# Seven matrix products that nobody reads, ahead of the first keys

## The chip, the cores and the metric

The kernel runs on one core of one Trainium2 chip. The metric is device time in microseconds (us). A profile of one execution goes with the times. TensorE (PE, with its weight loads as PEld), VectorE (DVE), ScalarE (ACT) and GpSimd (POOL) each have their own queue of instructions; SyncE (SP) mostly issues loads and stores.

## What is computed

The reference runs a decaying linear attention and then an FNet block, all in float32. Sizes are B = 4 batches, H = 8 heads, S = 768 positions, D = 64, so the model width is 512, and the MLP width is 2048.

```python
for b in range(nb):                       # blocks along the sequence
    intra = einsum('bhic,bhjc->bhij', qb, kb) * Dmask
    intra = einsum('bhij,bhjd->bhid', intra, vb)
    inter = einsum('bhid,bhde->bhie', qb * lam_pow, kv_state)
    out[:, :, sl] = intra + inter
    kv_state = lam_block * kv_state + einsum('bhsd,bhse->bhde', kb_dec, vb)
# x = out as (B, S, H*D)
mixed = real(fft(fft(x, axis=1), axis=2))
u = x + mixed
un = (u - mean) / sqrt(var + 1e-6)
y = u + maximum(un @ w_ch1, 0) @ w_ch2
```

`w_ch1` and `w_ch2` arrive as float64 and are turned into float32 on the chip.

## The kernel before

The work is written as Python generators that yield now and then; `weave` and `beside` run several of them side by side, so that the instructions of the attention, of the Fourier mixing, of the weight conversion and of the MLP are mixed in the program. A scheduler then orders the instructions of each engine by its own estimate of when things are ready. An instruction wrapped in `tc.keep_in_program_order` keeps its place. On each engine the instructions run in the order that results.

**Front.** The decay factor `lam` is loaded, an identity `ident` is built by GpSimd, and VectorE makes two tables out of them with scans: `decay` (L160, one scan for each of eight heads) and `qpow` (L167, four scans). Every score product is multiplied by `decay`.

**Attention.** A batch goes through six chunks of 128 positions. For each chunk `attn_in` (L259) loads k, q and v in pieces of 64 floats for one head and position, transposes k (L274) and q (L279) on TensorE against `ident`, and ScalarE copies the results out of PSUM as kT (L276) and qT (L281). GpSimd multiplies k by the decay (`kd`, L270); VectorE makes `qs` (L285). `attn_out` (L289) then multiplies kT and qT to scores (L298), VectorE applies the decay (`sc`, L302), the state gets kd times v (L315, and L317 or L320), and the output is summed from qs times the old state (L328) and sc times v (L332). ScalarE copies it out as `oT` (L335), TensorE turns it back (L348), and ScalarE writes x (L352, L353). The buffers of k, q and v are double, so a load waits until the chunk two before is used up. All the loads go through the sync queue, in order.

**Weights.** `load_weights` (L200) loads a piece of 512 columns of float64 as pairs of 32-bit words (`raw`, L209) and makes floats of it in seven instructions: two on ScalarE (L216, L218) and five on VectorE (L217, L220, L222, L224, L225). The two engines hand the piece to each other: L217 (VectorE), then L218 (ScalarE), then L220 (VectorE), and L216 (ScalarE) before L220. The pieces are woven between the chunks of batch 0 and the stages after it.

```python
pin(nc.scalar.activation(sg, top.bitcast(I16), AF.Sign))                      # L216
pin(nc.vector.tensor_scalar(pw, top, 0x7FF0, None, op0=ALU.bitwise_and))      # L217
nc.scalar.activation(pw, pw, AF.Relu, bias=cvt[:, 0:1], scale=8.0)            # L218
nc.vector.tensor_tensor(p, p, sg, op=ALU.mult)                                # L220
pin(nc.vector.tensor_scalar(d, hi, 0x000FFFFF, 0x00100000, ...))              # L222
nc.vector.scalar_tensor_tensor(dst, lo, 2.0 ** -32, d, ...)                   # L224
nc.vector.scalar_tensor_tensor(dst, dst, 2.0 ** -20, p, ...)                  # L225
```

**Mixing and MLP.** VectorE folds the rows (L426 to L484), TensorE does the two transforms (L516, then L529 to L534), VectorE adds the result to x (L596 to L600), takes mean and variance (L546, L547), GpSimd the power (L550, L551), and VectorE writes the normalised rows `un` (L564). TensorE transposes them (L569) and ScalarE copies them to `ut` (L570), the input of the MLP, whose first product is L633 and whose second is L647. The PSUM pool `pa` (five banks) serves the attention and the mixing; the pool `pm` (three banks), from which `psum_m` takes its tiles, serves the MLP alone. The later part of the MLP is computed with fewer products in a second phase (L720, L767).

The order of the main stages around the change is written in the last lines:

```python
run(part(att0, 2.7))
run(beside(att0, NC * t_chunk - 2.7, w, 0.25 * NW))
run(beside(part(mix, T_FOLD), T_FOLD, att1, 3.25 * t_chunk))
```

Of the kernel before, what the change touches and what calls it, by code (L numbers as in the profile page):

```python
# [76 lines left out]
def kernel(  # L77
# [10 lines left out]
    nc = tc.nc  # L88
# [50 lines left out]
    def new(pool, shape, tag, **kw):  # L139
        cnt[0] += 1  # L140
        return pool.tile(shape, F32, tag=tag, name=f"{tag}{cnt[0]}", **kw)
# [4 lines left out]
    def psum_m(shape):  # L146
        return new(pm, shape, "pm")
# [6 lines left out]
    ident = const.tile([128, 128], F32, name="ident")  # L154
# [17 lines left out]
    nc.gpsimd.memset(cvt, -896.0 * 16 * 8)  # L172
    mhalf = const.tile([128, G], F32, name="mhalf")
    nc.gpsimd.memset(mhalf, -0.5)

    st = [const.tile([128, HP, D], F32, name=f"st{i}") for i in range(2)]

# [725 lines left out]
```

## Time and profile before

| | |
|---|---|
| time, median of 3 | 826.14 us (825.62 to 828.82) |
| span of the profiled execution | 824.8 us |
| TensorE busy | 798.2 us |
| VectorE busy | 437.8 us |
| ScalarE busy | 186.5 us |
| first TensorE instruction | 4.68 us |
| first `oT` copy | 13.97 us |
| first normalised rows (`un`) | 91.99 us |

The first rows say how full each engine is over the whole run. A busy share of the whole run is a mean over stages that differ, so the stages are looked at one by one: the first 100 us hold attention, mixing and weight conversion, where several engines take part; after that TensorE has the MLP. The last three rows are marks in time by which two profiles can be compared.

### The profile page before, as it was taken

To read this page: it belongs to the slowest core of one execution; us is meant where nothing else is said; L and a number is where in the kernel's file an instruction comes from. 1 tells how busy PE (TensorE), PEld (TensorE's weight loads), DVE (VectorE), ACT (ScalarE), POOL (GpSimd) and SP (SyncE) were. 2 spreads that over 40 slices of the span, in tenths; PEclk is the share of its full clock that TensorE was granted. 3 is DMA by queue.
4 is the path that set the end of the run, shared out by engine and by line. 5 is a ranking of instruction groups with operands and counts; after the bars stand their busy time and mean duration, and the time that the engine had idled before them with its cause. 6 is when DMAs were issued, how large, how long until landed. Compare 5 with 4: busy or idle time off the path is not lost.

```text
span 824.8 us, 11701 instructions
## 1 busy us (share of the span) xinstructions
PE 798.2 (97%) x4608; PEld 637.5 (77%) x4608; DVE 437.8 (53%) x1018; ACT 186.5 (23%) x448; POOL 78.4 (10%) x102
## 2 busy tenths in 40 slices
PE   7989799999999999999999999999999999999998
PEld 5767675758575857768748888888888888888886
DVE  6899779685745571345895541155313561146311
ACT  3755243324521211212102210022001220012100
POOL 3123310011110110220100000000000000000000
PEclk9999899999999999999999999999999999999999
DMA  9969343238842137530442011100111001110010
GB/s 240 259 132 280 98 152 99 83 75 202 212 116 68 55 74 141 128 120 2 115 115 89 1 52 51 52 1 0 54 50 52 0 1 39 33 33 0 1 39 25
DMA packets 126684, 68.88 MB, mean 84 GB/s; under 512 B 111150, under 2 KB 112174, under 8 KB 126630
## 3 DMA queue, kind: packets, MB, share of 16 engines
q1 hardware_dynamic: 121488, 55.67, 26.6%
q0 software_dynamic: 2112, 6.69, 2.5%
q10 hardware_dynamic: 3030, 5.78, 2.0%
q8 instruction: 36, 0.59, 0.3%
q14 instruction: 18, 0.15, 0.1%
HBM read 48.72 MB, written 19.40 MB: 83 GB/s over the span
## 4 chain that ended last, share of the span: by engine, by line
PE 81%; DVE 9%; issue 4%; DMA 3%; ACT 2%; POOL 1%; POOLq 0%; ACTq 0%; DVEq 0%; SPq 0%
PE p L767 23%; PE p L720 23%; PE pm L647 10%; PE pm L633 8%; PE pa L332 3%; PE pa L298 3%; PE pa L516 3%; PE pa L328 2%; DMA raw<-in_moe_w_ch_dram 2%; PE pa L274 1%; PE pa L315 1%; PE pa L348 1%; PE pa L279 1%; DMA x<-xb,ix 1%; DVE sc L302 1%
## 5 line engine op out<-in xcount | busy, mean ns | idle before, releaser
L633 PE MATMUL pm<-ut,w 128*128 128x256 f32 x512 | 119.9, 383 | 0.0
L647 PE MATMUL pm<-w,hr 128*128 128x512 f32 x256 | 115.8, 597 | 0.6 <-DVE w L225 0.6
L633 PEld LDWEIGHTS pm<-ut,w 128*128 128x128 f32 x512 | 94.2, 190 | 15.8 <-issue 4.1
L720 PE MATMUL p<-ur,w 128*128 128x256 f32 x384 | 93.8, 379 | 0.0
L647 PEld LDWEIGHTS pm<-w,hr 128*128 128x128 f32 x256 | 46.7, 190 | 50.0 <-issue 47.8
L720 PEld LDWEIGHTS p<-ur,w 128*128 128x128 f32 x384 | 73.0, 190 | 10.3 <-issue 0.5
L720 PE MATMUL p<-us,w1s 128*128 128x256 f32 x256 | 65.7, 379 | 0.0
L767 PE MATMUL p<-w,hs 128*128 128x256 f32 x256 | 58.0, 379 | 0.5 <-DVE y L788 0.5
L767 PE MATMUL p<-w2s,hs 128*128 128x256 f32 x256 | 57.9, 379 | 0.0
L767 PE MATMUL p<-w,ha 128*128 128x256 f32 x256 | 57.9, 379 | 0.0
L767 PEld LDWEIGHTS p<-w,hs 128*128 128x128 f32 x256 | 48.5, 190 | 7.5 <-DVE y L788 0.9
L767 PEld LDWEIGHTS p<-w2s,hs 128*128 128x128 f32 x256 | 48.6, 190 | 6.6
L767 PEld LDWEIGHTS p<-w,ha 128*128 128x128 f32 x256 | 48.6, 190 | 6.6
L720 PEld LDWEIGHTS p<-us,w1s 128*128 128x128 f32 x256 | 48.6, 190 | 6.6
L747 ACT COPY ha<-p 128x256 f32<-128x256 f32 x32 | 11.9, 372 | 169.1 <-PE p L720 139.4
L622 POOL DMA_INDIRECT out_dram<-y,ix x12 | 11.8, 988 | 402.4 <-DVE y L793 341.6
L758 DVE TENSOR_TENSOR ha<-p,ha 128x256 f32<-128x256 f32 x32 | 13.6, 425 | 45.2 <-ACT ha L757 45.2
L298 PEld LDWEIGHTS pa<-qT,kT 64*128 64x128 f32 x384 | 26.8, 198 | 12.8 <-ACT qT L281 6.7
L302 DVE TENSOR_TENSOR sc<-pa,decay 128x512 f32<-128x512 f32 x48 | 31.5, 683 | 8.2 <-PE pa L298 8.2
L332 PE MATMUL pa<-sc,v 128*64 128x128 f32 x384 | 32.3, 286 | 3.1 <-DVE sc L302 3.0
L298 PE MATMUL pa<-qT,kT 64*128 64x128 f32 x384 | 31.5, 297 | 2.9 <-ACT qT L281 2.6
L720 PE MATMUL p<-us,w 128*128 128x256 f32 x128 | 32.9, 379 | 0.0
(144 smaller groups left out, 1122.1 us busy)
## 6 DMA issues: line engine op xcount, KB each, us to landing
raw<-in_moe_w_ch_dram SPq DMA_DIRECT2D x32, 512.0 KB, 4.6
k<-in_k_dram SPq DMA_DIRECT2D x24, 256.0 KB, 5.0
q<-in_q_dram SPq DMA_DIRECT2D x24, 256.0 KB, 5.9
v<-in_v_dram SPq DMA_DIRECT2D x24, 256.0 KB, 4.9
ud<-x SPq DMA_DIRECT2D x16, 256.0 KB, 2.3
utd<-e SPq DMA_DIRECT2D x64, 64.0 KB, 2.2
u<-ud SPq DMA_DIRECT2D x16, 256.0 KB, 2.7
ur<-utd SPq DMA_DIRECT2D x6, 512.0 KB, 4.4
```

The lines of the kernel that those rows point to most:

```text
L298: mm(pss[hi][:, hp, :], lhsT=kT[HD[hi], hp, :], rhs=qT[HD[hi], hp, :], start=True, stop=True)
L302: nc.vector.tensor_tensor(t, pss[hi], decay[:, hi::2, :], op=ALU.mult)
L328: mm(po[HD[hi], hp, :], lhsT=s_old[HD[hi], hp, :], rhs=qs[HD[hi], hp, :], start=(hp == 0), stop=False, skip_group_check=True)
L332: mm(po[HD[hi], hp, :], lhsT=vt[:, 2 * hp + hi, :], rhs=sc[hi][:, hp, :], start=(c == 0 and hp == 0), stop=(hp == HP - 1), skip_group_chec ...
L516: mm = nc.tensor.matmul(ps[0:m, n, :], lhsT=piece(a, i, n), rhs=cs[0:rows, a, i in (2, 3), n, :], start=(a == 0), stop=(a == 1))
L622: nc.gpsimd.indirect_dma_start(out=out.rearrange("b s d -> (b s) d"), out_offset=row_of(2 + HC * (b + 1) + T - HC), in_=y[:, :], in_offset ...
L633: nc.tensor.matmul(ps, lhsT=w1[:, c, 128 * fc:128 * fc + 128], rhs=ut[:, c, :], start=(c == 0), stop=(c == KO - 1))
L647: nc.tensor.matmul(ps, lhsT=hr[(fc - f0) // 4][:, fc % 4, 128 * i:128 * i + 128], rhs=w2[:, fc, :], start=(fc == f0), stop=(fc == f1 - 1))
L720: nc.tensor.matmul(ps, lhsT=s2.A[a][:, kt, 128 * i:128 * i + 128], rhs=U[b][:, kt, :], start=(first and kt == 0), stop=(kt == 1), skip_gro ...
L747: nc.scalar.copy(a11, two(X))
L758: V.tensor_tensor(a22, two(Z), a22, op=ADD)
L767: nc.tensor.matmul(ps, lhsT=h[a][:, s, i, :], rhs=s2.B[b][:, i, :], start=(first and i == 0), stop=(i == HF - 1), skip_group_check=True)
```

## The change

Ahead of the attention, TensorE is given seven products of the identity with itself. Their result goes to a PSUM tile of the MLP's pool and is read by nothing. The products keep their place in the program, ahead of the first transposes of the keys. They are meant for the time in which the first keys are still on their way and TensorE has nothing to do: the array is to be at its full clock when the keys come.

```diff
     mhalf = const.tile([128, G], F32, name="mhalf")
     nc.gpsimd.memset(mhalf, -0.5)
+
+
+    idle = psum_m([128, 128])
+    for _ in range(7):
+        tc.keep_in_program_order(nc.tensor.matmul(idle, lhsT=ident, rhs=ident, start=True, stop=True))
 
     st = [const.tile([128, HP, D], F32, name=f"st{i}") for i in range(2)]
```

The diff shows all that was written. The scheduler decides the rest: with the seven products in the program it also places many other instructions of the first 117 us elsewhere, on all engines. After L174 the line numbers of the changed kernel are higher by five.

## The prediction

> **What bounds the kernel now.** I read the engine totals first, then the windows by stage, then the chain of waits and the timelines of the front. On the page:
>
> ```profile
> PE 798.2 (97%) x4608; PEld 637.5 (77%) x4608; DVE 437.8 (53%) x1018; ACT 186.5 (23%) x448; POOL 78.4 (10%) x102
> ```
>
> TensorE is busy for 798.2 of 824.8 us, so at most 26.6 us of idle time, plus slow matmuls, can be gained at all. The windows by stage say where:
>
> ```profile
> 20.00:40.00 20.00, 18.26 (x228) 15.17 (x227) 17.25 (x33) 14.24 (x33) 4.64 (x5) 1.00 1.02 258
> 40.00:60.00 20.00, 17.50 (x213) 13.79 (x214) 19.65 (x40) 11.92 (x30) 4.20 (x4) 1.00 0.72 152
> 80.00:120.00 40.00, 34.77 (x258) 28.14 (x257) 29.74 (x70) 16.87 (x40) 10.06 (x12) 0.91 0.45 132
> ```
>
> The columns are span, length, busy time of PE, PEld, DVE, ACT, POOL, then clock, DMA share, GB/s. Between 20 and 60 us VectorE is as full as TensorE (17.25 and 19.65 of 20 us), so a faster TensorE alone gives little there. From about 94 us, when the MLP has its first input, TensorE nearly always has work. A front that ends earlier pays only by what it moves the first normalised rows, at 91.99 us. The chain of waits in the front:
>
> ```profile
> 0.73 3.82 DMA k<-in_k_dram
> 4.55 0.14 issue
> 4.68 1.08 PE pa L274 x4
> 5.80 1.13 PE pa L279 x4
> 6.95 0.59 ACT qT L281
> 7.59 2.08 PE pa L298 x16
> 9.67 1.05 PE pa L315 x16
> 10.72 0.42 PE pa L332 x2
> 11.14 1.05 PE pa L274 x4
> 12.19 1.76 PE pa L332 x14
> 13.97 0.58 ACT oT L335
> ```
>
> It is TensorE nearly alone, and slow: L298 takes 2.08 us here and 1.16 at 15.71 us, L332 x14 1.76 against 1.10 at 19.16. Single L332 records shrink from 421 to 273 ns near 13.5 us. The page prints clock 1.00 in this stretch, so the durations, not that column, show that the array starts slow.
>
> **What the Trainium skill says.** "TensorE: Matmul & The Clock Gate", section "Part 1: The HAM clock gate", says that the array starts at half clock, that a busy window of about 3413 ns releases it, and that the windows run free of the kernel's start. This trace agrees: clock 0.50 from 92.14 to 98.97 us (6.83 us, two such windows), and counting windows of 3.413 us back from 98.97 gives 13.63, 10.22, 6.81 and 3.39 us, where 13.63 fits the shrinking records. The window 6.81 to 10.22 was some 80% busy (gap 6.91 to 7.59) and released nothing; 10.22 to 13.63 was full and did. The same page, under "Architectural detail", has ScalarE and VectorE as strict FIFO, which every step below uses; ScalarE standing 4.20 us at a weight word (shown below) agrees. "DMA: Bandwidth & Descriptors", section "Specifications", asks 512 B or more for line rate; 111150 of the 126684 packets here are under that, so the loads of the front are slow to land.
>
> **The change, part by part.** Line numbers are those of before.
>
> Added: seven f32 products of 128x128. A plain f32 product is two records (L529: two per call), 0.43 us at the low clock (L529 x2 at 95 us), so 7 x 0.43 = 3.0 us. They wait only for the identity (GpSimd, done at 1.67 us) and so run from about 1.7 to 4.75 us, beside the k load that ends at 4.55. The k transposes start perhaps 0.07 us later; that is hidden, since the q transposes wait for their own load until 5.79. Their PSUM buffer is first wanted at 100 us: nothing.
>
> Gained at the front: TensorE is now busy from 1.7 to 6.9 us, so the full window 3.39 to 6.81 releases the clock 6.8 us earlier. Then qT is copied at about 6.5, L298 runs 7.1 to 8.3. VectorE is busy with the scans until 6.99+2.16 = 9.15 us, so the first score product moves only from 9.70 to 9.15. The second ends at 10.45, k transposes fit before it, and L332 x14 ends at 11.7 instead of 13.95. ScalarE then has to fit L218 before oT, so VectorE's L220 comes at 13.5 instead of 15.22: 1.7 us gained. Bounds: 1.1 (release late) to 2.2 (TensorE's own gain).
>
> Moved: the scheduler orders much of the first 117 us anew; after that the built orders agree but for few places. Three moves matter.
>
> (1) VectorE's L217 on the third weight word goes ahead of L224 and qs of the third chunk. That word lands late:
>
> ```profile
> 21.19 0.69 DVE L224 SCALAR_TENSOR_TENSOR w<-raw,w 128x512 f32<-128x512 uint32 x1
> 21.98 0.69 DVE L285 TENSOR_TENSOR qs<-pa,qpow 128x512 f32<-128x512 f32 x1
> 22.80 0.67 ACT L216 ACTIVATE e<-raw 128x512 bf16<-128x512 int16 x1 [0.31 <-DMA raw<-in_moe_w_ch_dram]
> ```
>
> It lands at 22.74 us. Its issue, in the sync queue behind a v load, can move up by at most 1.1 us (that load waits from 12.83 to 13.96 for TensorE), with the DMA share near 1 all the while. So it lands at 21.6 to 22.7, VectorE stands there for 2 us or more, and behind it queue L224, qs, L225, L220, L222, sc, L224: with the step from the landing some 4.0 us to the second sc, at 25.7 to 26.7 us against 25.39. The gain of 1.7 us is spent, and 0.3 to 1.3 us more. TensorE's L328 and L332 wait for that.
>
> (2) Later in batch 0 other words are converted earlier, and k transposes and kT go ahead of oT. By the last chunk VectorE has 4.67-2.56 = 2.1 us less left between second sc and qs, so the lag is made up: about level, give or take 0.6 us, at 52 us.
>
> (3) The weight load that stands at 61.18 us is put ahead of the v load that held it in the queue:
>
> ```profile
> 60.70 0.37 SPq L263 DMA_DIRECT2D v<-in_v_dram  x1
> 61.18 0.52 SPq L209 DMA_DIRECT2D raw<-in_moe_w_ch_dram  x1
> 67.12 0.66 ACT L216 ACTIVATE e<-raw 128x512 bf16<-128x512 int16 x1 [4.20 <-DMA raw<-in_moe_w_ch_dram]
> 67.69 0.57 ACT L335 COPY oT<-pa 128x512 f32<-128x512 f32 x1
> 68.31 0.66 PE L348 MATMUL pa<-ident,oT 128*128 128x128 f32 x4 [1.04 <-ACT oT L335]
> ```
>
> It can now issue at 57.5 and land at 57.5+5.9 = 63.4. ScalarE no longer holds oT from 66.25 to 67.69: 1.4 us. VectorE's L217 for it now stands before the scores and may wait some 0.3 us, and VectorE's folds then bind, with 2.6 us of work from L470 to the next scores. I credit 0.8 us.
>
> Sum at the first normalised rows: level after (2), less 0.8, and 0.3 for small idle times of VectorE that close (0.46 at 20.2, 0.75 at 79.5 us): 1.1 us earlier. 826.14 - 1.1 = 825.0 us.
>
> **The rivals.**
>
> A, the front gain is spent and the rest is small: 825.0 (824 to 826.5). For it: VectorE full from 20 to 60 us. Against: that same VectorE idles 3.01 us before 15.22, which the change does attack.
>
> B, faster by over 0.5%. The weight word lands as early as VectorE wants it, so the 1.7 us last, and 0.8 comes at 68. Besides, TensorE now idles from 88.25 to 92.55 us, one whole window (88.73 to 92.14) lies in it, and the clock falls:
>
> ```profile
> 88.25:92.50 4.25, 0.01 (x1) 0.00 (x0) 3.32 (x9) 0.80 (x3) 1.29 (x2) 0.96 1.12 272
> 92.50:99.00 6.50, 5.94 (x34) 5.35 (x34) 2.56 (x7) 1.67 (x5) 3.14 (x3) 0.50 0.35 95
> ```
>
> From 94.15 to 98.97 the chain is TensorE, 4.8 us at half clock. If the moved idle no longer covers a window, half of that goes: 2.4 us. 826.1 - 1.7 - 0.8 - 2.4 = 821.2. Against: three things must go well.
>
> C, the words land late at further places where L217 now stands earlier (fourth and fifth chunk): 0.5 us at each of three, so about 827.6.
>
> D, slower by over 0.5%: the 1.3 us of step (1) stays, and stalls open one more idle window of 3.41 us in which nothing comes to TensorE: 826.1 + 1.3 + 3.4 = 830.8. Against: 18.26 of 20 us are busy from 20 to 40 us.
>
> **How the numbers follow.** A 0.55, C 0.12, B 0.22, D 0.11. A is the likeliest: 825.0. Same is A and C, 0.67; faster 0.22; slower 0.11. The range 821.0 to 829.5 cuts about half of B and most of D, which is the 2 in 10.
>
> **What would show it.** In the changed profile 14 identity records from 1.7 to 4.8 us; L298 of the first chunk near 1.2 us long; oT of the first chunk about 1 us earlier or more; ScalarE's L216 or VectorE's L217 waiting for a weight word near 21 to 23 us; ScalarE's wait of 4.20 us before 67 us gone or short; the first un within 2 us of 91.99. I am wrong if L298 stays at 2 us (no release), if VectorE does not stand near 22 us (B), or if the half-clock stretch at 92 us is gone.

## The result, and the profile after

The changed kernel takes 830.78 us (median of 6; 829.41 to 835.1) against 825.81 us for the kernel before beside it: ratio 1.0063, 95% interval 1.0036 to 1.0091. It is slower by about 5 us, where 1 us faster was forecast. Of all executions below one, of e1 at 1378.73 us with a mean clock of 0.56, was in a slow state and is left out of its ratio. Line numbers of the changed kernel are higher by five, so L303 below is L298 of before, L307 is L302 (`sc`), L222 is L217.

The engine totals of the changed kernel, and its windows by stage (span, length, busy time of PE, PEld, DVE, ACT, POOL, clock, DMA share, GB/s):

```profile
PE 803.4 (97%) x4622; PEld 641.8 (77%) x4622; DVE 439.7 (53%) x1018; ACT 186.8 (23%) x448; POOL 78.7 (9%) x102
```

```profile
20.00:40.00 20.00, 17.08 (x212) 13.84 (x212) 16.98 (x34) 14.19 (x33) 4.59 (x4) 1.00 0.98 251
40.00:60.00 20.00, 17.93 (x208) 14.06 (x206) 19.03 (x38) 11.55 (x29) 3.35 (x4) 1.00 0.63 138
80.00:120.00 40.00, 34.56 (x263) 28.66 (x262) 28.56 (x66) 18.14 (x44) 8.54 (x11) 0.91 0.45 125
```

From 20 to 40 us TensorE does 16 matmuls fewer than in the kernel before and is busy 1.2 us less. The chain of waits in the front of the changed kernel:

```profile
1.22 4.93 DMA q<-in_q_dram
6.15 0.04 issue
6.19 1.13 PE pa L284 x4
7.32 0.02 issue
7.34 0.59 ACT qT L286
7.94 0.04 issue
7.98 2.13 PE pa L303 x16
```

The 14 identity records run from 1.73 us and delay nothing: the chain goes past them, to the load of q. But L303 takes as long as L298 did, 2.1 us, so the array is still slow at 10 us. Further on, VectorE from 20 us (start, duration, engine, line, operation, and the wait before it), and last the second `sc` of this chunk in the kernel before:

```profile
20.07 0.41 DVE L227 TENSOR_SCALAR w<-raw 128x512 uint32<-128x512 uint32 x1
22.36 0.43 DVE L222 TENSOR_SCALAR e<-raw 128x512 uint16<-128x512 uint16 x1 [1.87 <-DMA raw<-in_moe_w_ch_dram]
22.70 0.68 DVE L229 SCALAR_TENSOR_TENSOR w<-raw,w 128x512 f32<-128x512 uint32 x1
23.30 0.68 DVE L290 TENSOR_TENSOR qs<-pa,qpow 128x512 f32<-128x512 f32 x1
...
26.64 0.68 DVE L307 TENSOR_TENSOR sc<-pa,decay 128x512 f32<-128x512 f32 x1
```

```profile
25.39 0.68 DVE L302 TENSOR_TENSOR sc<-pa,decay 128x512 f32<-128x512 f32 x1
```

That is the forecast wait, and the second `sc` at 26.64 us, in the foreseen 25.7 to 26.7. The weight load that stood at 61.18 us, and ScalarE behind it, also went nearly as foreseen: ScalarE's wait of 4.20 us is 0.43 (lines of the timeline, sync queue and ScalarE).

```profile
58.66 0.81 SPq L214 DMA_DIRECT2D raw<-in_moe_w_ch_dram  x1
...
64.87 0.67 ACT L221 ACTIVATE e<-raw 128x512 bf16<-128x512 int16 x1 [0.43 <-ACT x L358]
```

What was not foreseen comes after. These are windows of the changed kernel, cut at the clock's own borders (its records have the clock released at 11.00 us, and half from 75.86 to 79.27 us and from 96.34 to 103.16 us):

```profile
4.18:7.59 3.41, 3.03 (x13) 2.04 (x11) 3.41 (x10) 0.83 (x2) 0.72 (x1) 1.00 1.18 266
7.59:11.00 3.41, 3.02 (x33) 2.79 (x34) 2.18 (x5) 0.34 (x1) 0.36 (x1) 1.00 1.34 251
72.44:75.86 3.42, 1.73 (x18) 1.32 (x19) 3.42 (x9) 0.83 (x2) 0.47 (x2) 1.00 1.06 304
75.86:79.27 3.41, 3.41 (x14) 3.31 (x14) 2.80 (x6) 1.69 (x4) 3.28 (x1) 0.50 0.82 173
```

A window in which TensorE was busy for 1.73 of 3.41 us, VectorE for all of it, was followed by one at half clock. TensorE stood there for VectorE (timeline of the changed kernel, and last the same `sc` in the kernel before):

```profile
71.70 1.27 DVE L484 TENSOR_TENSOR fo<-fo 65x255 f32<-65x255 f32 x1
72.90 0.41 DVE L485 TENSOR_TENSOR fo<-fo 65x255 f32<-65x255 f32 x1
73.23 1.28 DVE L307 TENSOR_TENSOR sc<-pa,decay 128x512 f32<-128x512 f32 x2
...
73.97 0.43 PE L337 MATMUL pa<-sc,v 128*64 128x128 f32 x2 [1.57 <-DVE sc L307]
```

```profile
71.14 1.28 DVE L302 TENSOR_TENSOR sc<-pa,decay 128x512 f32<-128x512 f32 x2
```

The lag, mark by mark, with four of the experiments below (each column is one profiled execution; us against the profile of before):

| mark (time before) | change | e7, change again | e2 | e3 | e12 |
|---|---|---|---|---|---|
| scores of the second chunk (15.71) | -0.66 | -1.93 | -0.42 | -1.89 | -1.76 |
| first `sc` of batch 1 (52.56) | +1.19 | +2.21 | +2.00 | +0.45 | -0.27 |
| `sc` of its fourth chunk (71.14) | +2.09 | +3.12 | +2.92 | +1.36 | +0.31 |
| first `un` (91.99) | +3.97 | +3.32 | +3.12 | +1.57 | +0.51 |

So the front is early at 16 us, as foreseen but by less in this profile, late at 52 us, where level was foreseen, and later still at 72 and 92 us.

### The profile page after: what moved, and what is told of

Read it like the earlier page. It is cut to its first block, busy times and chain, and to the rows that moved or that the text cites. A ratio compares the mean times of both kernels' runs of the same rounds, so it can differ in the third digit from the quotient of the medians.

```text
span 829.6 us, 11732 instructions
## 1 busy us (share of the span) xinstructions
PE 803.4 (97%) x4622; PEld 641.8 (77%) x4622; DVE 439.7 (53%) x1018; ACT 186.8 (23%) x448; POOL 78.7 (9%) x102
## 4 chain that ended last, share of the span: by engine, by line
PE 78%; DVE 10%; DMA 4%; issue 4%; ACT 2%; POOL 1%; SPq 0%; POOLq 0%; ACTq 0%; DVEq 0%
PE p L772 23%; PE p L725 23%; PE pm L652 9%; PE pm L638 8%; PE pa L521 3%; PE pa L337 3%; PE pa L303 2%; DMA raw<-in_moe_w_ch_dram 2%; PE pa L333 1%; PE pa L353 1%; PE pa L279 1%; DVE sc L307 1%; DMA x<-xb,ix 1%; DVE w L229 1%; PE pa L320 1%
## 5 line engine op out<-in xcount | busy, mean ns | idle before, releaser
L303 PEld LDWEIGHTS pa<-qT,kT 64*128 64x128 f32 x384 | 27.3, 198 | 12.0 <-ACT qT L286 6.2
L307 DVE TENSOR_TENSOR sc<-pa,decay 128x512 f32<-128x512 f32 x48 | 31.4, 683 | 7.5 <-PE pa L303 7.4
L303 PE MATMUL pa<-qT,kT 64*128 64x128 f32 x384 | 32.0, 298 | 2.1 <-ACT qT L286 2.1
L337 PEld LDWEIGHTS pa<-sc,v 128*64 128x64 f32 x384 | 23.1, 136 | 13.4 <-DVE sc L307 7.5
```

The source lines that it names most:

```text
L303: mm(pss[hi][:, hp, :], lhsT=kT[HD[hi], hp, :], rhs=qT[HD[hi], hp, :], start=True, stop=True)
L307: nc.vector.tensor_tensor(t, pss[hi], decay[:, hi::2, :], op=ALU.mult)
L337: mm(po[HD[hi], hp, :], lhsT=vt[:, 2 * hp + hi, :], rhs=sc[hi][:, hp, :], start=(c == 0 and hp == 0), stop=(hp == HP - 1), skip_group_chec ...
```

## The experiments

**Theory.** The products cost nothing by themselves; the new order costs, where conversion work and its waits stand ahead of the decay products `sc`. **Rival 1**: work of TensorE ahead of the keys costs by itself, through the clock. **Rival 2**: the half-clock window at 76 us is all of it. Times are medians; each kernel was measured beside the kernel before on the same chip, and the ratio is to that. The kernel before had 825.81 (change), 826.50 (e1 to e4), 826.21 (e5 to e7), 826.39 (e8 to e11) and 826.64 us (e12 to e14), so times from different groups can differ by 0.8 us for the chip alone.

| run | us | ratio (95% interval) |
|---|---|---|
| e1 work, old order | 829.29 | 1.0037 (1.0024 to 1.0050) |
| e2 one product | 829.79 | 1.0045 (1.0032 to 1.0058) |
| e3 third piece pinned | 828.51 | 1.0030 (1.0016 to 1.0044) |
| e4 narrow products | 826.18 | 0.9996 (0.9986 to 1.0007) |
| e5 tile alone | 826.30 | 1.0009 (0.9997 to 1.0021) |
| e6 float32 products, old order | 826.84 | 1.0009 (0.9997 to 1.0022) |
| e7 change again | 832.56 | 1.0075 (1.0048 to 1.0101) |
| e8 18 products, old order | 827.92 | 1.0023 (1.0012 to 1.0033) |
| e9 e8 and third piece pinned | 827.47 | 1.0016 (1.0004 to 1.0028) |
| e10 third piece pinned alone | 825.97 | 0.9996 (0.9985 to 1.0006) |
| e11 e1 again | 827.75 | 1.0017 (1.0005 to 1.0029) |
| e12 all pieces pinned, change | 827.81 | 1.0019 (1.0007 to 1.0032) |
| e13 all pieces pinned, one product | 826.15 | 0.9993 (0.9980 to 1.0006) |
| e14 all pieces pinned, no product | 825.74 | 0.9986 (0.9978 to 0.9994) |

**Work without the new order: e1, e4.** Products of another size leave every engine's order as it was before.

```diff
+    warm = const.tile([128, 128], BF16, name="warm")
+    nc.vector.memset(warm, 0.0)
...
-    for _ in range(7):
-        tc.keep_in_program_order(nc.tensor.matmul(idle, lhsT=ident, rhs=ident, start=True, stop=True))
+    for _ in range(28):
+        tc.keep_in_program_order(nc.tensor.matmul(idle[:, 0:128], lhsT=warm, rhs=warm[:, 0:128], start=True, stop=True))
```

> The identity products are left out; in their place TensorE runs 28 bfloat16 products of a tile of zeros, about as long (28 records against 14 of twice the length), which a memset on VectorE readies. Every engine's order is that of the kernel before but for these added instructions. Theory (the products cost nothing, the order costs): ratio 0.998 to 1.001, that is 824 to 826.5 us. Rival 1 (work of TensorE ahead of the keys costs by itself, by late transposes or by the clock): 829 to 831 us. Rival 2 (the half-clock window at 76 us alone makes the time): 825.8 us as well, since 76 us follows from stalls that this order doesn't have.

e4 is the changed kernel with `idle[:, 0:4]` and `ident[:, 0:4]` for `idle` and the second `ident`.

> The seven products with 4 columns each instead of 128: TensorE starts on them as early, but is busy for a small part of the time; every engine keeps the order of the kernel before. Theory (order costs): 825.5 to 826.2 us, no change. Rival 1: 825.8 to 827 us, a small part of the cost. Rival 2: 825.8 us.

e4 is level. It was meant to have short products, but its trace shows that they are hardly shorter: the 14 records with 4 columns take 3.15 us, those with 128 columns 3.35, and the weight loads between them have 333 ns at the median in both. So e4 has nearly the changed kernel's work on TensorE in the old order, and the time stays; the clock was released at 13.47 us in its profile, at 13.63 in that of before. e1 is a miss for the theory. Its front was level (`un` at 91.81 us); in the profiled execution VectorE got a gathered x late at 371 us, TensorE stood, and a half-clock window followed from 374.6 to 378.0 us; VectorE's marks go from 0.5 us early at 125 us to 2.0 us late at 383 us. Whether that belongs to the products was open. Its five other executions have 3.4 half-clock windows on average (counted as below), the kernel before beside them 1.9.

**The order without the work: e2.** One product instead of seven (`range(1)`), which already brings an order much like the changed one.

> One product of the identity in place of seven: no warm array, and an order of instructions that has the early weight load and the fold order of the changed kernel, but not VectorE's early L222 on the third weight word. Theory (the order costs): 827 to 829.5 us, slower than before by 0.2 to 0.4%, without any work on TensorE to speak of. Rival 1 (the work of seven products costs): 825.8 us, as before. Rival 2 (the half-clock window at 76 us): slower only if its profile shows half clock near 76 us.

829.79 us, and 3.12 us late at `un` with the clock at full from 12.43 to 94.35 us. So most of the loss comes from the order, with one product and without a half-clock window at 76 us: rival 2 falls as the whole cause, and rival 1 for the larger part.

**The wait for the third word: e3.** The length of `late_words` says for how many of the first weight pieces the three instructions marked `pin` keep their place in the program; those of later pieces go where the scheduler puts them.

```diff
-    late_words = [0, 1]
+    late_words = [0, 1, 2]
```

> The changed kernel with the three pinned instructions of a weight piece kept for the third piece too, so that VectorE's L222 no longer stands ahead of qs of the third chunk. Theory (the wait for the third weight word costs 1.3 to 2 us and the fold order near 72 us the rest): 828.5 to 829.5 us, 1.3 to 2 us under the changed kernel; the 1.87 us wait at 22 us is gone. Rival 1 (the work of the products costs): 830.8 us, unchanged. Rival 2 (half clock at 76 us alone): 830.8 us if it is still there, 827.4 us if not.

828.51 us, 2.3 us under the changed kernel. The lag at the first `sc` of batch 1 shrinks from 1.19 to 0.45 us. The wait was not gone but shared: 0.65 us for the third word and 2.08 us for the fourth; but right behind them now stand the two `sc` of the third chunk, with no conversion work before them. Behind that chunk the order isn't mended: four and six conversion instructions stand between `qs` and the first `sc` in the fourth and fifth. This run also shows the forecast front, as its clock was released at 7.00 us (TensorE in e3):

```profile
7.89 1.16 PE L303 MATMUL pa<-qT,kT 64*128 64x128 f32 x16 [0.68 <-ACT qT L286]
8.98 0.69 PE L320 MATMUL pa<-v,kd 128*64 128x64 f32 x16
9.83 0.43 PE L337 MATMUL pa<-sc,v 128*64 128x128 f32 x2 [0.16 <-DVE sc L307]
...
13.82 1.16 PE L303 MATMUL pa<-qT,kT 64*128 64x128 f32 x16 [0.45 <-ACT qT L286]
```

**The products in float32 in the old order, and the change once more: e5, e6, e7.** e5 has the tile as `[128, 64]` float32 with its memset, and no product. e6 adds, with the tile `idle` of the change,

```diff
+    for _ in range(14):
+        tc.keep_in_program_order(nc.tensor.matmul(idle[0:64, 0:64], lhsT=warm, rhs=warm, start=True, stop=True))
```

> No products. The kernel before with the extra tile of e1 and its memset on VectorE, 256 bytes a partition, which moves the tiles after it; every order as before. If the 2.8 us that e1 lost come from its tile (memory or the memset): 828 to 830 us. If they come from TensorE's work ahead of the keys, or from chance: 825.5 to 826.5 us, with a mean clock of 0.996 to 0.998 in nearly all executions.

> The tile of e5, and 14 float32 products of 64x64 of it (about the 3 us of the seven of 128x128), in the order of the kernel before. Theory (order alone costs): 825 to 826.5 us, un at 91.5 to 92. Rival 1 (work ahead of the keys costs in itself, as e1 suggests): 828 to 830 us, un still near 92 and the loss after it, with a mean clock of 0.994 or less in most executions.

> The changed kernel once more, for the phase of the clock's windows. Theory (order: 1.2 us at 52 us, 2.1 us at 73 us, and a half-clock window at 76 us in some executions): 829.5 to 831.5 us; un at 94 to 94.5 us if no window before 80 us is at half clock, at 95.5 to 96.5 us if one is. Rival 2 (the half-clock window makes all of it): under 827.5 us in executions without one.

e5 clears the tile. e6 is level within its interval, and 0.5 us above e5. Rival 1 then has at most a small part in e6's form. e6's profile is of its slowest execution, 830.73 us, with half clock from 74.34 us and `un` at 95.18, where 91.5 to 92 was expected: the old order can have such an execution too. e7 repeats the change, at 832.56 us, and its profile has no half clock at 76 us, yet is 3.32 us late at `un`. It has half clock elsewhere: from 23.89 us, after the wait for the third word, and from 303.78 us. Its windows:

```profile
20.47:23.88 3.41, 1.02 (x22) 0.86 (x22) 1.98 (x4) 1.99 (x5) 0.00 (x0) 1.00 1.07 239
23.88:27.30 3.42, 3.42 (x35) 2.64 (x32) 3.42 (x7) 0.97 (x3) 1.06 (x1) 0.50 1.03 243
71.67:75.09 3.42, 1.85 (x36) 1.50 (x34) 3.42 (x7) 0.66 (x1) 1.18 (x1) 1.00 0.86 281
300.37:303.78 3.41, 1.82 (x24) 1.16 (x25) 3.33 (x10) 0.00 (x0) 2.06 (x3) 1.00 0.24 42
```

The same stall of TensorE near 72 us falls here into windows otherwise (1.85 us busy), and the clock stays. So where a half-clock window comes depends on how the stalls lie against windows that differ from execution to execution; that this alone decides it isn't shown. Their number follows from the mean clock of an execution: (1 - clock) x span / (0.5 x 3.413). Over the 12 executions of the change and e7:

| half-clock windows | executions | us |
|---|---|---|
| 2 | 3 | 828.77, 829.41, 830.07 |
| 3 | 2 | 830.17, 831.40 |
| 4 | 2 | 831.38, 831.47 |
| 5 | 3 | 832.43, 833.66, 834.35 |
| 6 | 2 | 834.67, 835.10 |

From 829.41 (middle of 2) to 834.9 (mean of 6) is 1.4 us a window. That is a slope over executions, which doesn't part the slow window from the stall that brings it; over the one at 303.78 us in e7 VectorE's lag grows by 1.6 us (3.05 at 275 us, 4.66 at 321). The kernel before has 2.1 windows on average (59 executions beside e12 to e14), the change 3.9.

**A longer warm-up, and e1 again: e8 to e11.** e8 is e6 with `range(18)`, e9 adds the pin of e3 to it, e10 is the kernel before with that pin alone.

> e6 with 18 products instead of 14, so that TensorE is busy from 1.0 us until the keys are there, about 5.1 us, and on to 6.9 or 7.2 us; every order as before. A full window of the clock then lies ahead of the scores in most executions. Theory (the early clock is real and the old order can keep part of it): clock released by 7.2 us in the profile in 7 of 10 cases, second chunk's scores near 13.9 us instead of 15.7, un 0.5 to 1.5 us earlier, 825 to 826 us. Rival (the front is set by the weight words and the loads): the scores of the second chunk are early but un is level, 826 to 826.5 us.

> e8, and the third weight piece pinned in program order as well: both decay products of the third chunk then stand ahead of that piece's L220 and L222 in the old order. If the VectorE work ahead of the second decay product sets the front: 824 to 825.5 us, the best of all. If the front is set elsewhere: as e8.

> The kernel before with that pin alone, no products. Its orders differ from before by eight places on VectorE and more on TensorE. If any other order than the one before costs: 827 us or more. If it is the waits of the changed order that cost: 825.5 to 826.5 us.

> e1 once more. If its 2.8 us were chance in few executions (extra half-clock windows): 826 to 827.5 us, like e6. If its bfloat16 products cost: 828.5 to 829.5 us again.

e8 and e11 are slower by 0.23 and 0.17%, with the old order. Against the theory's first half, that the products cost nothing, stand 1.4 to 1.5 us in these two forms; e6 is 0.6 us above the 826.21 us of before beside it, within its interval. In e8's profile the clock was released at 6.80 us and the second chunk's scores came at 14.23 instead of 15.71; but then TensorE stood 0.92 us for a load of q at 20.27 us and VectorE 0.83 us for the third weight word at 23.67 us, and half-clock windows followed from 27.28 and from 75.07 us. An early start meets loads that don't come earlier. In e9's the clock rose at 4.24 us, after a window full of products, and fell again at 7.65 us after one that was 1.92 us busy, so that the early release was lost at once; 824 to 825.5 us were expected of it. Half-clock windows are more frequent (2.4, 2.3 and 2.4 on average in e8, e9 and e11, 1.9 to 2.0 in the kernel before beside these and e4), but 0.3 to 0.5 windows at 1.4 us are 0.5 to 0.6 us, not 1.5. e8's executions with one window and those with two have medians of 827.65 and 828.01 us, those of the kernel before beside it 825.64 and 826.40. The traces, one for each kernel, show a place for the rest, and no cause: near 370 us VectorE waits for a gathered x for 4.59 us in e1, 4.09 in e6, 4.18 in e8 and 4.00 in e9, and its marks fall back by 1.4 to 2.0 us there against those of before. In e11 it waits 2.90 us; in all other profiles 2.5 to 2.7. Only kernels with both the tile `warm` and products on it have the long wait. As e4 has such work without the tile and is level, the 1.5 us are not shown to come from work on TensorE. e10, which changes few places on VectorE, is level: another order doesn't cost because it is another.

**Undoing the order's fault: e12 to e14.** The pin for all pieces that are woven into batch 0:

```diff
-    late_words = [0, 1]
+    late_words = list(range(8))
```

With it `sc` stands ahead of most of the conversion work in the third to sixth chunk. e12 has the seven products, e13 one, e14 none.

> The changed kernel, seven products and all, with the pinned instructions of every weight piece woven into batch 0 kept in program order: the decay products of the third to sixth chunk then stand ahead of most conversion work (none to two conversion instructions between qs and the first of them, up to three more ahead of the second). Theory (conversion work and waits ahead of the decay products cost the 3.3 us of e2): un at 91.5 to 93 us, 826 to 828 us, so 3 us or more under the changed kernel. Rival 1 (the work of the seven products, through the clock): 829.5 us or more, no better than e3.

> One product, and the same pins. Against e12 the rest that the work of seven products costs by itself. Theory: 825.5 to 826.5 us, 3 us or more under e2; e12 higher than this by 0.5 to 1.5 us, as e6, e8 and e11 stand to the kernel before. If the order of the folds in batch 1 mattered as much as the conversion: 827.5 us or more is excluded here, since this order has the folds as before; then e12 would be 1 us or more higher than e13 for that.

> The kernel before with these pins and no product. If the decay products' place sets the front: 824.5 to 826 us, at or under the kernel before; un at 90.5 to 92 us. If the pins cost elsewhere (words converted later, the MLP waiting): 827 us or more, and e12 can't be read as an undoing.

The fifth chunk on VectorE, from `qs` to the second `sc`: first the changed kernel, then e12.

```profile
36.92 0.69 DVE L290 TENSOR_TENSOR qs<-pa,qpow 128x512 f32<-128x512 f32 x1 [0.96 <-ACT qT L286]
37.52 0.42 DVE L227 TENSOR_SCALAR w<-raw 128x512 uint32<-128x512 uint32 x1
38.09 0.43 DVE L225 TENSOR_TENSOR e<-e 128x512 bf16<-128x512 bf16 x1 [0.15 <-ACT e L223]
38.44 0.69 DVE L229 SCALAR_TENSOR_TENSOR w<-raw,w 128x512 f32<-128x512 uint32 x1
39.04 0.69 DVE L307 TENSOR_TENSOR sc<-pa,decay 128x512 f32<-128x512 f32 x1
39.64 0.68 DVE L230 SCALAR_TENSOR_TENSOR w<-w,e 128x512 f32<-128x512 f32 x1
40.24 0.68 DVE L307 TENSOR_TENSOR sc<-pa,decay 128x512 f32<-128x512 f32 x1
```

```profile
35.63 0.69 DVE L290 TENSOR_TENSOR qs<-pa,qpow 128x512 f32<-128x512 f32 x1 [0.23 <-ACT qT L286]
36.24 0.42 DVE L222 TENSOR_SCALAR e<-raw 128x512 uint16<-128x512 uint16 x1
37.37 0.69 DVE L307 TENSOR_TENSOR sc<-pa,decay 128x512 f32<-128x512 f32 x1 [0.71 <-PE pa L303]
37.97 0.41 DVE L225 TENSOR_TENSOR e<-e 128x512 bf16<-128x512 bf16 x1
38.30 0.42 DVE L227 TENSOR_SCALAR w<-raw 128x512 uint32<-128x512 uint32 x1
38.64 0.68 DVE L307 TENSOR_TENSOR sc<-pa,decay 128x512 f32<-128x512 f32 x1
```

In the changed kernel three conversion instructions and a wait for ScalarE stand between `qs` and the first `sc`; in e12 one does, and the first `sc` waits for TensorE instead, so VectorE no longer holds it. e12 takes 827.81 us, 3 us under the change and 4.8 under e7 (on other chips), and its first `sc` of batch 1 is 0.27 us early where the change was 1.19 and 2.21 us late. e13 is level with before, 3.6 us under e2. e14, at 0.9986, beats the kernel before a little: the lowest median measured here belongs to a kernel with no products at all. The pins are worth about 1 us by themselves, then, so that of the 3.6 us between e2 and e13 somewhat under 3 undo the new order's fault. e13's executions with two half-clock windows have a median of 824.57 us, those with three 827.23; the kernel before beside it has 826.38 with two. e12 stays 1.7 us above e13. Of that 0.8 us is there at `un` (92.50 against 91.74), where e12 also keeps the changed order of the folds and e13 doesn't; and e12 has 3.1 half-clock windows, e13 2.7.

## Why the prediction was wrong

**Added products: right on the path, wrong on the whole.** 14 records from 1.73 us, 3.35 us where 3.0 were forecast, hidden beside the loads; k's transposes at 4.98 us waited for k, which landed later here. In the old order kernels with such work lost nothing (e4), 0.5 (e6 against e5, within the intervals) or 1.5 us (e8), by half-clock windows in part and, in the profile, at the gathered x near 370 us, with the cause left open.

**"The full window 3.39 to 6.81 releases the clock": wrong in the profile, right in e3 and e7.** The windows' phase was counted back from the profile of before and used for another execution. "TensorE: Matmul & The Clock Gate", section "Part 1: The HAM clock gate", says that the windows run free of the kernel; I cited it and then used one phase. The releases here agree with it: 11.00 us in the change, 6.82 in e7, 7.00 in e3, 5.94 in e12. Where it came early, the second chunk's scores came 1.8 to 1.9 us earlier, the forecast 1.7; in the profile shown above, 0.66.

**Move (1): right.** VectorE stood 1.87 us at the third weight word (2.36 in e7), and the second `sc` was 1.25 us late, in the forecast 0.3 to 1.3.

**Move (2), "the lag is made up ... about level, give or take 0.6 us, at 52 us": this step failed.** It was 1.19 us late there, 2.21 in e7, 2.00 in e2. I had counted how much VectorE work remained between the second `sc` and `qs` and not where the rest went: in the fourth to sixth chunk one to three conversion instructions went between `qs` and the first `sc`, where none stood, and three or four ahead of the second, where two stood; and TensorE waits for `sc`. The sixth chunk on VectorE, before and changed:

```profile
44.70 0.68 DVE L285 TENSOR_TENSOR qs<-pa,qpow 128x512 f32<-128x512 f32 x1
45.30 0.68 DVE L302 TENSOR_TENSOR sc<-pa,decay 128x512 f32<-128x512 f32 x1
45.89 0.41 DVE L217 TENSOR_SCALAR e<-raw 128x512 uint16<-128x512 uint16 x1
46.23 0.41 DVE L222 TENSOR_SCALAR w<-raw 128x512 uint32<-128x512 uint32 x1
46.56 0.68 DVE L302 TENSOR_TENSOR sc<-pa,decay 128x512 f32<-128x512 f32 x1
```

```profile
44.37 0.68 DVE L290 TENSOR_TENSOR qs<-pa,qpow 128x512 f32<-128x512 f32 x1
44.97 0.41 DVE L222 TENSOR_SCALAR e<-raw 128x512 uint16<-128x512 uint16 x1
...
45.76 0.69 DVE L307 TENSOR_TENSOR sc<-pa,decay 128x512 f32<-128x512 f32 x1
46.77 0.43 DVE L225 TENSOR_TENSOR e<-e 128x512 bf16<-128x512 bf16 x1 [0.31 <-ACT e L223]
...
47.71 0.68 DVE L307 TENSOR_TENSOR sc<-pa,decay 128x512 f32<-128x512 f32 x1
```

At `qs` the lag was made up, as forecast: 44.37 against 44.70 us (in e7 and e2, with 45.20 and 45.39, not wholly). But part of the work that was gone ahead of `qs` now stood behind it, and the second `sc` was 1.15 us late. e12 and e13 show it by undoing it; e3 mends the third chunk alone and still goes from 0.87 us early at this `qs` (43.83) to 0.44 late at this `sc` (47.00).

**Move (3): the load and ScalarE right, the credit of 0.8 us wrong.** The scores at 69.36 us had caught up to +0.24, but the `sc` after them fell back from +1.52 in the chunk before to +2.09 us, since VectorE had one fold more ahead of it, L484, and that at 1.27 us beside GpSimd's `kd`; in the kernel before that `kd` ran beside the `sc` themselves, which took their usual 1.28 us. The text said that VectorE's folds then bind and credited half of the gain all the same. From 52 to 71 us the lag grew by 0.90 us in the change and by 0.91 in e7 and 0.92 in e2, where 0.8 less was forecast.

**The half clock: the rule in rival B, that the idle must cover a window, was too narrow, and the sum of the central case had no term for new half-clock windows.** Windows with TensorE busy for 1.02 to 1.92 us were followed by half clock; others of 1.54 to 1.87 us were not. In the changed kernel's profile the lag grew from 2.09 to 3.97 us between 71 and 92 us, with the half-clock window at 76 us; in e7, without one there, by 0.20 us. Rival D came nearest: a lag that stays, and stalls that bring more. That it gives 830.8 us, the measured median, is luck in part. Its 1.3 us of lag were 3.3 us of order (e2), and its 3.4 us were a whole window with nothing for TensorE; neither profile of the change has one more of these ahead of `un` than the kernel before. What came was a stall of 1.57 us and 1.8 half-clock windows more than before, at 1.4 us each. Its argument against, that 18.26 of 20 us are busy, was a mean over 20 to 40 us: the stall near 72 us lies behind that, and e7's at 20.47 us fills only one window in it.

## What to carry to other kernels

With a scheduler in between, a small insertion is a new order: compare the orders, and where they differ ask for each wait what newly stands ahead of the instruction that the busiest engine waits for; a sum of work that still fits doesn't answer that. Try an insertion in the old order too, and the new order without the insertion; here the new order alone cost 3.3 us of about 5, and kernels with the work alone between nothing and 1.5 us. Read the trace of such a control, too: the narrow products of e4 were not shorter. A warm array was worth something here only where the stage that followed kept it busy; where another engine set the pace, the gain was spent before it arrived, and in e9 the clock fell again at once.

## What the hardware showed beyond what was expected

- Half clock does not need a TensorE that is idle for a whole window. After 1.46 us busy of 3.41 (e8, 27.28 us), 1.55 (e1, 374.62 us), 1.73 (change), 1.80 (e8, 75.07 us), 1.82 (e7, 303.78 us) and 1.92 (e9, 7.65 us) it fell; after 1.54 (e1, 825.18 us), 1.59 (e5, 90.73 us), 1.74 (change, 24.66 us), 1.83 (before, 300.36 us), 1.85 (e7, e12) and 1.87 (e3) it didn't. Between 1.5 and 1.9 us both happen, so the busy time of the profile, whose matmul ends are modelled, doesn't decide it alone; what else does is open.
- A window of 3.03 us busy released nothing (4.18 to 7.59 us of the change, products and transposes), while 3.02 us of the next did, and 3.35 us in e3. In e4 3.33 us released nothing (3.23 to 6.64 us, four-column products and transposes), in e8 3.34 us did (3.39 to 6.80 us). The busy time of the profile isn't quite what the clock goes by.
- A VectorE fold of 65x255 takes 0.41 us alone and 1.27 us beside GpSimd's `kd` (71.53 to 72.70 us in the change); the same happened in e2 and e3 at the same place.
- Float32 products with 4 columns instead of 128 were hardly shorter at the low clock: 354 against 421 ns a record at the median, and 14 of them 3.15 against 3.35 us (e4, change), each behind a weight load of 128 columns.
